# Two attentions on one core: the log-sum rows, spread by VectorE instead of copied by a transfer

## The chip, the cores and the metric

The kernel runs on one core of one Trainium2 chip. The metric is the device time of one execution in microseconds; of several executions the median counts.

## The reference

Two attention layers, A and B, each over its own input x (1 x 2048 x 1024) with its own weights wqkv (1024 x 3072) and wo (1024 x 1024), 32 heads of 32. The results stand side by side in the output.

```python
# A: 8 keys, every second position back          # B: the last 256 positions
off = jnp.arange(8) * 2                          mask = (idx[:, None] - idx[None, :] >= 0) & \
idx = pos[:, None] - off[None, :]                       (idx[:, None] - idx[None, :] < 256)
logits = einsum("bhsd,bhswd->bhsw", q, kg) * scale
attn = softmax(where(mask, logits, -1e9)); o = einsum("bhsw,bhswd->bhsd", attn, vg)
return concatenate([a @ wo_A, b @ wo_B], axis=-1)
```

All is float32. The kernel reaches that precision with matmuls of a shorter format (fp32r) by splitting a number into a high and a low part and adding three products (hi x hi, hi x lo, lo x hi).

## The kernel before, in words

**Units and head groups.** The work is cut into 8 units of 512 positions: four of B ("dense", 256 keys back) and then four of A (its even and odd positions apart, so that its keys are a window of 8 neighbours). Each unit has 8 head groups of 4 heads, 64 head groups in all. The host only lays the arrays out.

**Gemm.** For each unit: q and k of each head group (`qk_items`, matmuls of line 412), the values (`v_items`, line 464) and the output projection (`o_items`, line 510). A weight of 512 KB comes in by a transfer that GpSimd issues (line 137) and is split by VectorE into its two parts (lines 163 and 171) before TensorE reads it.

**Stacked queries and keys.** A finished q or k is evacuated by ScalarE (line 349) and VectorE (line 353) into `nat`, and six transfers issued by SyncE (line 373) place its parts in `qst` and `kst`. There each of the 4 heads has 96 partitions: 32 dimensions times the three pairs of parts, so that one matmul over 96 partitions gives a full-precision score. Two such pairs of tiles alternate between head groups.

**First pass.** Sixteen matmuls a head group (line 681, 4 blocks of 128 queries by 4 heads) give scores with the queries on the partitions. VectorE takes each row's maximum (line 686) and ScalarE the sum of the exponentials (line 691). When all sixteen are done, ScalarE takes the logarithm (line 704), and VectorE makes the negative log-sum and splits it into two parts, `hl` (lines 709 to 712).

**The rows.** The matmul of line 720 turns `hl` round: 32 rows by 128 positions, 16 of high parts and 16 of low parts, row 4j+b (and 16+4j+b) for head j and query block b. VectorE copies them to `rt` (line 724), and a transfer issued by SyncE (line 727) lays them in partitions 96 and 97 of `qst`. `kst` holds ones there, written once at the start (line 285).

**Second pass.** Matmuls over 98 partitions (line 763 in dense units, 566 in the others) give scores with the keys on the partitions, with the log-sum already subtracted by the two extra rows, so that ScalarE's exponential (lines 770 and 573) is the finished softmax. GpSimd or VectorE masks it (lines 749, 752, 583), and the matmuls of lines 810 and 607 multiply by the values. The result is split into `ot` (lines 644 and 648).

**What sets the order.** Nothing is scheduled on the chip. While the program is built, a planner (`Clock`) keeps for each engine the time at which it comes free, books each instruction with a cost written down in the code, and takes from four lists (the rows matmul `aux`, second pass and values `twos`, first pass `ones`, gemm) the item that is ready first, in that order where two are. Each engine then runs its instructions in the order so found, and real semaphores make it wait where the plan was too early. For a transfer the planner books the issue, a move and a tail:

```python
LEAD = dict(sp=1.34, act=0.97, pool=1.43)
MOVE = dict(load=(2.12, 0.14), store=(0.64, 0.4), copy=(1.18, 0.56), rows=(0.37, 0.56), ...
```

A head group's first pass is due when its keys have landed (`done["stack"]`, line 361), its second pass when `h["rows"]` has (line 728). The last step of a q or k gemm waits for an earlier `nat` to be placed, which in turn waits for the second pass of the head group two before, since the stacked tiles are shared. The four PSUM banks of the scores (`rs`) are shared by both passes and the rows.

Of the kernel before, what the change touches and what calls it, by code (L numbers as in the profile page):

```python
# [7 lines left out]
F32 = mybir.dt.float32  # L8
F32R = mybir.dt.float32r
AF = mybir.ActivationFunctionType  # L10
ALU = mybir.AluOpType
# [3 lines left out]
P = 128  # L15
# [6 lines left out]
NRAW, NP, NO, NS = 3, 768, 10, 4  # L22
POOL_BIAS = -99
MASK_BIAS = 0.2
VPARTS = ((0,2),(2,2),(4,2),(6,2))
V_SLOTS = {0: 0, 1: 1, 5: 2, 7: 3}
O_SLOTS = {2: (0, 1), 3: (2, 3), 4: (4, 5), 5: (6, 7)}
V0_SLOTS = {0:0,2:1,4:2,7:3}
NX, NST, NN = 9,1,3
TAIL, XAT = 4, 1  # L30
C1, C3, CG, CV = 0.108, 0.2, 0.231, 0.242
TERMS = ((0, 0), (0, 1), (1, 0))
# [2 lines left out]
class Clock:  # L35
# [4 lines left out]
    SEEN = dict(act=0.15, dve=0.115, pool=0.08)  # L40
    LEAD = dict(sp=1.34, act=0.97, pool=1.43)
    HOLD = dict(sp=0.63, act=0.35, pool=0.6)
    MOVE = dict(load=(2.12, 0.14), store=(0.64, 0.4), copy=(1.18, 0.56), rows=(0.37, 0.56),
                halo_out=(0.4, 0.68), halo_in=(0.55, 0.6), halo_few=(0.28, 0.51))

    def __init__(self):
# [134 lines left out]
def kernel(ctx, tc, xs, wqk, wv, wo, outs, units):  # L181


    nc = tc.nc
    U = len(units)
    ctx.enter_context(tc.manual_schedule())
    const = ctx.enter_context(tc.tile_pool(name="const", bufs=1))
# [6 lines left out]
    small = ctx.enter_context(tc.tile_pool(name="small", bufs=2))  # L194
# [6 lines left out]
    ck = Clock()  # L201
# [28 lines left out]
    for p in plan:  # L230
# [3 lines left out]
        elif p[0] == "v":  # L234
            s0, n = VPARTS[p[2]]
# [25 lines left out]
    def constants():  # L261
        def bands(name, n, keep, fill, *conds):
            m = const.tile([P, n], F32, name=name) if isinstance(name, str) else name
            nc.gpsimd.memset(m, keep)
            for step, base, chan in conds:
                nc.gpsimd.affine_select(m, m, pattern=[[step, n]], compare_op=ALU.is_ge, fill=fill, base=base,
                                        channel_multiplier=chan)
            return m

        ident = cst["ident"] = const.tile([P, P], F32R, name="ident")  # L270
        keep = const.tile([P, P], F32, name="keep_d")
        nc.gpsimd.memset(keep, 0.0)
        nc.gpsimd.affine_select(ident, keep, pattern=[[-1, P]], compare_op=ALU.not_equal, fill=1.0, base=0,
                                channel_multiplier=1)
        cst["mask_d"] = bands("mask_d", 384, 0.0, FAR, (1, -1, -1), (-1, 256, 1))
        cst["mask_w"] = bands("mask_w", 136, 0.0, FAR, (1, -1, -1), (-1, 8, 1))
        cst["keep_f"] = bands("keep_f", P, BIG, 0.0, (-1, -1, 1))
        cst["keep_d"] = bands(keep, P, BIG, 0.0, (1, 0, -1))
        cst["keep_w"] = bands("keep_w", 136, BIG, 0.0, (1, 0, -1), (-1, 7, 1))
        ck.use("pool", 3.0, ck.now)  # L280

        def ones():
            zero = cst["mask_d"][96:98, None, P:2 * P].to_broadcast([2, 24, P])
            for t in kst:
                nc.scalar.activation(t[96:98, :, :].rearrange("p j (a s) -> p (j a) s", s=P), zero, AF.Identity,
                                     bias=1.0, scale=1.0)
                ck.use("act", 2.7, ck.now)

        ck.defer(13.0, ones)
# [39 lines left out]
    def latest(*ts):  # L329
        return None if any(t is None for t in ts) else max(ts)  # L330


    def qk_items(u, s):
# [12 lines left out]
        def evac(t, ps, bank):  # L346
            hl = natp.tile([P, 2, S], F32R, tag="nat", name="nat")
            sc = SCALE if t == 0 else 1.0
            nc.scalar.activation(hl[:, 0, :], ps, AF.Copy, scale=sc)  # L349
            r = ck.use("act", 0.485, ck.now + ck.SEM)  # L350

            def low():
                nc.vector.scalar_tensor_tensor(hl[:, 1, :], ps, sc, hl[:, 0, :].bitcast(F32), op0=ALU.mult,  # L353
                                               op1=ALU.subtract)
                e = ck.use("dve", 0.61, r)
                rg.give(bank, e)

                def stack():
                    e2 = place(1, e)
                    if t == 1:  # L360
                        done["stack"][u, s] = max(e2, h2["hi"])
                    if t == 1 and u + 1 < U and units[u + 1][3]:
                        nc.sync.dma_start(halo[u % 2][s], hl[:, :, 256:].bitcast(F32))
                        e2 = ck.copy("halo_out", e, ck.now)
                    done["nat"][hg, t] = max(e2, h2["hi"])

                later(stack)

            def place(part, e):
                dst, c = (qst[buf], 0) if t == 0 else (kst[buf], 256)  # L370
                for i, a in enumerate((0, 0, 1) if t == 0 else (0, 1, 0)):
                    if a == part:
                        nc.sync.dma_start(dst[i:96:3, :, c:c + S].bitcast(F32), hl[:, a, :].bitcast(F32))
                        e2 = ck.copy("copy", e, ck.now)
                return e2

            def stack_hi():
                if t == 0 and has_halo:
                    read_halo()
                h2["hi"] = place(0, r)  # L380

            def later(f):
                if hg < 2 or hg - 2 in done["second"]:
                    f()
                else:
                    waiting.setdefault(hg - 2, []).append(f)

            h2 = {}
            later(stack_hi)
            ck.defer(r, low)  # L390
# [155 lines left out]
    def window(u, s, h):  # L546
# [12 lines left out]
        def second(ki, hp):  # L559
            kb, q0, n, pack = kbs[ki]  # L560
            if hp == 0:
                h["left", ki] = 4 // pack
            ps, bank = rs.take()
            for i in range(pack):
                j = hp * pack + i
                nc.tensor.matmul(ps[:, i * n:(i + 1) * n], kk[0:98, j, 256 + kb * P:256 + (kb + 1) * P],  # L566
                                 q[0:98, j, q0:q0 + n], start=True, stop=True)
            w = pbuf[:, hp * pack:hp * pack + pack, at[ki]:at[ki] + n]
            if ki == nk - 1 and hp == 4 // pack - 1:
                free_keys(hg)  # L570

            def expo():
                nc.scalar.activation(w, ps[:, :pack * n].rearrange("p (j n) -> p j n", j=pack), AF.Exp)  # L573
                e = ck.use("act", pack * n / 1200 + 0.055, ck.now, pfree[0])
                rs.give(bank, e)

                def masks():
                    if kb < 0:
                        nc.gpsimd.affine_select(w, w, pattern=[[0, pack], [-1, n]], compare_op=ALU.is_ge, fill=0.0,
                                                base=-121, channel_multiplier=1)  # L580
                        r = ck.use("pool", 0.21, e)
                    else:
                        nc.vector.tensor_tensor(w, w, cst["keep_w"][:, None, :n].to_broadcast([P, pack, n]),  # L583
                                                op=ALU.min)
                        r = ck.use("dve", pack * n / 960 + 0.07, e, port=True)
                    h["left", ki] -= 1
                    h["pr", ki] = max(h.get(("pr", ki), 0.0), r)

                ck.defer(e - 0.1, masks)

            return expo
# [25 lines left out]
        def seconds(ki):  # L617
            pack = kbs[ki][3]
            for hp in range(4 // pack):
                two.append(Item(lambda: latest(rs.when(), h["rows"]),  # L620
                                lambda ki=ki, hp=hp: second(ki, hp), pack * C1))

        for ki in range(nk):
# [32 lines left out]
    def attention(u, s):  # L656
# [61 lines left out]
        def rows(hl):  # L718
            ps, bank = rs.take()
            nc.tensor.matmul(ps[0:32, 0:P], hl.rearrange("p a b -> p (a b)"), cst["ident"], start=True, stop=True)  # L720
            rt = small.tile([32, P], F32R, tag="rt", name="rt")

            def copy():
                nc.vector.tensor_copy(rt, ps[0:32, 0:P])
                e = ck.use("dve", 0.2, ck.now)
                rs.give(bank, e)
                nc.sync.dma_start(q[96:98, :, :].bitcast(F32), rt.bitcast(F32))
                h["rows"] = ck.copy("rows", e)

            return copy  # L730

        for b in range(4):
            for j in range(4):
# [21 lines left out]
        def second(ki, hp):  # L755
# [4 lines left out]
                h["left", ki, pr] = 2 // pack  # L760
            ps, bank = rs.take()
            for i, j in enumerate(heads):
                nc.tensor.matmul(ps[:, i * n:(i + 1) * n], kk[0:98, j, 256 + kb * P:256 + (kb + 1) * P],  # L763
                                 q[0:98, j, q0:q0 + n], start=True, stop=True)
            w = pbuf[:, heads[0]:heads[0] + pack, at[ki]:at[ki] + n]
            if ki == nk - 1 and hp == 4 // pack - 1:
                free_keys(hg)
# [20 lines left out]
        def second_ready(ki, hp):  # L788
            pack = kbs[ki][3]
            pr = hp * pack // 2  # L790
            if lot[ki] and ("pv", 0) not in h:
                return None
            return latest(rs.when(), h["rows"])

        def values_ready(ks):
            if ks[-1] == nk - 1 and hg >= NO and ((hg - NO) // NG, NG - 1) not in done["out"]:
# [146 lines left out]
```

## Time and profile before

| What | us |
|---|---|
| median of 3 timed runs | 1946.54 (1946.42 to 1950.07) |
| the profiled execution | 1951.22 |
| its span | 1949.5 |
| TensorE busy | 1904.4 |
| VectorE busy | 1261.6 |
| ScalarE busy | 960.6 |
| GpSimd busy | 375.8 |

The granted TensorE clock was 0.995. The span is what the profiler's records cover; the execution's own time lies 1.7 us above it. Engines: PE is TensorE, PEld its weight loads, DVE VectorE, ACT ScalarE, POOL GpSimd, SP SyncE. A row of the waits names who waited, at which line, for whom, and gives the total, the number of times and the longest. A row of the timeline gives start, duration, engine, line, operation and tiles; the bracket is the idle time ahead of it and what ended it. A row of groups gives the count, then busy time and the mean of one in ns. The records of matmuls that follow each other overlap (a matmul of 512 columns is recorded with 398 ns, while three take 0.74 us), so that an idle time of less than about 0.2 us between two matmuls does not show.

### The profile page before, as it was taken

What the parts mean: (1) busy time and instruction counts of PE and PEld (TensorE: products, weight loads), DVE (VectorE), ACT (ScalarE), POOL (GpSimd) and SP (SyncE); (2) the same over time, 40 slices, a digit from 0 to 9 for tenths busy, and PEclk for the clock granted to TensorE, in tenths of its full rate; (3) what the DMA queues carried; (4) which work ended last, traced back from release to release, by engine and by line L of the source; (5) the groups of instructions that cost most, each with busy time, mean ns of one, the idle gap of its engine ahead of it and who ended that gap; (6) DMA issues with size and microseconds to landing.
All of it is one profiled execution on the core that took longest, in us unless ns stands there. A gap on an engine that the chain in (4) does not pass through costs nothing. (4 is left out here: it accounts for less than half of the span.)

```text
span 1949.5 us, 35937 instructions
## 1 busy us (share of the span) xinstructions
PE 1904.4 (98%) x12608; PEld 1608.6 (83%) x12608; DVE 1261.6 (65%) x3733; ACT 960.6 (49%) x3136; POOL 375.8 (19%) x958
## 2 busy tenths in 40 slices
PE   8999999999999999999999999999999999999999
PEld 6787787788877888778878888888888788888887
DVE  6667566667666676666755667656676566765673
ACT  3555565655565656565655333433444343434441
POOL 1222222323332323232431001000010000000010
PEclk9999999999999999999999999999999999999999
DMA  6456555455545464555454556545564556546451
GB/s 200 131 141 174 134 147 166 136 150 174 144 141 166 133 185 120 144 147 144 134 147 118 173 164 188 157 133 169 148 182 128 169 158 174 167 130 176 138 157 66
DMA packets 136500, 294.90 MB, mean 151 GB/s; under 512 B 14464, under 2 KB 42112, under 8 KB 136320
## 3 DMA queue, kind: packets, MB, share of 16 engines
q1 hardware_dynamic: 85632, 124.82, 26.0%
q0 software_dynamic: 40320, 146.82, 23.2%
q10 hardware_dynamic: 10368, 20.98, 3.0%
q8 instruction: 100, 1.64, 0.4%
q14 instruction: 80, 0.66, 0.1%
HBM read 163.58 MB, written 27.26 MB: 98 GB/s over the span
## 5 line engine op out<-in xcount | busy, mean ns | idle before, releaser
L412 PE MATMUL g<-x,w 128*128 128x512 f32 x3072 | 799.2, 398 | 9.3 <-DVE w L163 9.0
L412 PEld LDWEIGHTS g<-x,w 128*128 128x128 f32 x3072 | 556.9, 189 | 109.3 <-DVE w L163 10.2
L691 ACT ACTIVATE s<-s,nm 128x384 f32<-128x384 f32 (+3 forms) x1024 | 452.2, 442 | 269.1 <-DVE nm L686 261.0
L464 PE MATMUL g<-w,x 128*128 128x256 f32 x3072 | 411.8, 285 | 0.0
L464 PEld LDWEIGHTS g<-w,x 128*128 128x128 f32 x3072 | 392.9, 192 | 2.0 <-issue 0.2
L686 DVE CUSTOM_DVE_ANT_0 s<-s,mask_d 128x384 f32<-128x384 f32 (+2 forms) x512 | 262.4, 555 | 188.5 <-PE s L681 187.7
L510 PE MATMUL g<-ot,w 128*128 128x512 f32 x1416 | 356.7, 396 | 2.7 <-ACT ot L644 2.3
L171 DVE TENSOR_TENSOR w<-raw,w 128x512 fp32r<-128x512 f32 x502 | 328.0, 695 | 8.7
L510 PEld LDWEIGHTS g<-ot,w 128*128 128x128 f32 x1416 | 258.5, 189 | 53.6 <-ACT ot L644 3.3
L749 POOL TENSOR_SCALAR_AFFINE_SELECT pbuf<-pbuf 128x128 f32<-128x128 f32 (+1 forms) x643 | 219.0, 372 | 296.9 <-ACT pbuf L770 295.8
L681 PE MATMUL s<-kst,qst 96*128 96x384 f32 (+3 forms) x1024 | 232.6, 302 | 15.7 <-DMA kst<-nat 9.7
L770 ACT ACTIVATE pbuf<-s 128x384 f32<-128x384 f32 (+2 forms) x480 | 201.9, 503 | 65.8 <-PE s L763 62.6
L681 PEld LDWEIGHTS s<-kst,qst 96*128 96x128 f32 x1024 | 178.4, 190 | 55.6 <-issue 18.2
L686 DVE CUSTOM_DVE_ANT_0 s<-s,mask_w 128x136 f32<-128x136 f32 (+1 forms) x512 | 142.0, 321 | 113.2 <-PE s L681 112.8
L691 ACT ACTIVATION_READ_ACCUMULATOR s<-s,nm 128x1 f32 x1024 | 209.9, 205 | 0.0
L349 ACT ACTIVATE nat<-g 128x512 fp32r<-128x512 f32 x128 | 76.6, 599 | 249.7 <-PE g L412 245.4
L137 POOL DMA_DIRECT2D raw<-wqk x126 | 68.0, 540 | 572.7 <-DVE w L171 218.2
L353 DVE SCALAR_TENSOR_TENSOR nat<-g,nat 128x512 fp32r<-128x512 f32 x128 | 88.3, 690 | 139.1 <-ACT nat L349 136.2
L163 DVE CAST w<-raw 128x1024 fp32r<-128x1024 f32 x251 | 173.1, 690 | 7.3 <-DMA raw<-wqk 7.3
L686 DVE DVE_READ_ACCUMULATOR2_ANT nm<- 128x1 f32 x1024 | 143.7, 140 | 0.0
L763 PEld LDWEIGHTS s<-qst,kst 98*128 98x128 f32 x704 | 109.0, 189 | 40.4 <-ACT s L691 19.6
L583 DVE TENSOR_TENSOR pbuf<-pbuf,keep_w 128x272 f32<-128x272 f32 (+1 forms) x224 | 95.5, 471 | 70.1 <-ACT pbuf L573 69.8
(53 smaller groups left out, 1071.3 us busy)
## 6 DMA issues: line engine op xcount, KB each, us to landing
raw<-wqk POOLq DMA_DIRECT2D x126, 512.0 KB, 3.7
qst<-nat SPq DMA_DIRECT2D x192, 256.0 KB
kst<-nat SPq DMA_DIRECT2D x192, 256.0 KB
raw<-wo POOLq DMA_DIRECT2D x64, 512.0 KB, 3.7
raw<-wv POOLq DMA_DIRECT2D x62, 512.0 KB, 3.7
raw<-xs POOLq DMA_DIRECT2D x28, 512.0 KB, 4.7
outs<-ost ACTq DMA_DIRECT2D x56, 256.0 KB
halo<-nat SPq DMA_DIRECT2D x40, 256.0 KB
```

What stands on the lines that cost most here:

```text
L163: nc.vector.tensor_copy(t[:, 0, :], raw)
L171: nc.vector.tensor_tensor(o, a, b, op=ALU.subtract)
L412: nc.tensor.matmul(h["ps"], h["w"][:, a, k * P:(k + 1) * P], xt[u][k][:, b, :], start=(k == 0 and i == 0), stop=(k == NK - 1 and i == 2))
L464: nc.tensor.matmul(ps, xt[u][k][:, a, p0:p0 + P], h["w"][:, c, k % kw], start=(k == 0 and i == 0 and r == 0), stop=(k == NK - 1 and i == 2 ...
L510: nc.tensor.matmul(h["ps"], w[:, a, c:c + P], ot[u, k][:, b, :], start=(k == 0 and i == 0), stop=(k == NK - 1 and i == 2))
L583: nc.vector.tensor_tensor(w, w, cst["keep_w"][:, None, :n].to_broadcast([P, pack, n]), op=ALU.min)
L681: nc.tensor.matmul(ps[:, :n], q[0:96, j, b * P:(b + 1) * P], kk[0:96, j, c0:c1], start=True, stop=True)
L686: nc.vector.tensor_tensor_reduce(ps[:, :n], ps[:, :n], mask[:, cut:full], scale=-1.0, scalar=BIG, op0=ALU.add, op1=ALU.min, accum_out=nm)
L691: nc.scalar.activation(ps[:, :n], ps[:, :n], AF.Exp, bias=nm, scale=-1.0, accum_out=sm)
L749: nc.gpsimd.affine_select(w, w, pattern=[[0, m], [step, n]], compare_op=ALU.is_ge, fill=0.0, base=base, channel_multiplier=chan)
L763: nc.tensor.matmul(ps[:, i * n:(i + 1) * n], kk[0:98, j, 256 + kb * P:256 + (kb + 1) * P], q[0:98, j, q0:q0 + n], start=True, stop=True)
L770: nc.scalar.activation(w, ps[:, :pack * n].rearrange("p (j n) -> p j n", j=pack), AF.Exp)
```

## The change

VectorE no longer copies the 32 rows, and the transfer is gone. In its place stand four multiplications, one a head, that write 32 rows of `qst` each: all 32 rows of the matmul's result, repeated over the 4 query blocks, times a small table `pick` that is 1 where a row belongs to the head and the block and 0 elsewhere. `kst` holds ones in 32 partitions instead of 2, and the second pass runs over all 128 partitions. The second pass of a head is due in the plan when that head's multiplication is done, instead of when all rows have landed. `ROWS_LATE`, added to that time, is 0. `KEYS_LATE` adds 1.2 us to the time at which the planner takes the keys to have landed. As the planner's times change, so does the order of the instructions on every engine.

```diff
+ROWS_LATE, KEYS_LATE = 0, 1.2
...
+        pick = cst["pick"] = const.tile([32, 16], F32, name="pick")
+        nc.gpsimd.memset(pick, 0.0)
+        for row in (0, 16):
+            nc.gpsimd.affine_select(pick, pick, pattern=[[-1, 16]], compare_op=ALU.not_equal, fill=1.0, base=-row,
+                                    channel_multiplier=1)
...
-            zero = cst["mask_d"][96:98, None, P:2 * P].to_broadcast([2, 24, P])
+            zero = cst["mask_d"][96:P, None, P:2 * P].to_broadcast([32, 24, P])
             for t in kst:
-                nc.scalar.activation(t[96:98, :, :].rearrange("p j (a s) -> p (j a) s", s=P), zero, AF.Identity,
+                nc.scalar.activation(t[96:P, :, :].rearrange("p j (a s) -> p (j a) s", s=P), zero, AF.Identity,
...
-                        done["stack"][u, s] = max(e2, h2["hi"])
+                        done["stack"][u, s] = max(e2, h2["hi"]) + KEYS_LATE
...
-                nc.tensor.matmul(ps[:, i * n:(i + 1) * n], kk[0:98, j, 256 + kb * P:256 + (kb + 1) * P],
-                                 q[0:98, j, q0:q0 + n], start=True, stop=True)
+                nc.tensor.matmul(ps[:, i * n:(i + 1) * n], kk[:, j, 256 + kb * P:256 + (kb + 1) * P],
+                                 q[:, j, q0:q0 + n], start=True, stop=True)
...
-                two.append(Item(lambda: latest(rs.when(), h["rows"]),
+                two.append(Item(lambda hp=hp: latest(rs.when(), h["rows"] and h["rows"][hp * pack + pack - 1]),
...
-            rt = small.tile([32, P], F32R, tag="rt", name="rt")
-
-            def copy():
-                nc.vector.tensor_copy(rt, ps[0:32, 0:P])
-                e = ck.use("dve", 0.2, ck.now)
+            def spread():
+                h["rows"] = []
+                for j in range(4):
+                    nc.vector.tensor_tensor(q[96:P, j, :].rearrange("p (b s) -> p b s", s=P),
+                                            ps[0:32, None, 0:P].to_broadcast([32, 4, P]),
+                                            cst["pick"][0:32, 4 * j:4 * j + 4, None].to_broadcast([32, 4, P]), op=ALU.mult)
+                    e = ck.use("dve", 0.61, ck.now)
+                    h["rows"].append(e + ROWS_LATE)
                 rs.give(bank, e)
-                nc.sync.dma_start(q[96:98, :, :].bitcast(F32), rt.bitcast(F32))
-                h["rows"] = ck.copy("rows", e)
```

The dense second pass is changed in the same two places.

More of the change, by code (lines that the diff above doesn't have):

```diff
@@ L28 @@
 V0_SLOTS = {0:0,2:1,4:2,7:3}
-NX, NST, NN = 9,1,3
+NX, NST, NN = 9, 1, 3
 TAIL, XAT = 4, 1
@@ L42 @@
     HOLD = dict(sp=0.63, act=0.35, pool=0.6)
-    MOVE = dict(load=(2.12, 0.14), store=(0.64, 0.4), copy=(1.18, 0.56), rows=(0.37, 0.56),
+    MOVE = dict(load=(2.12, 0.14), store=(0.64, 0.4), copy=(1.18, 0.56),
                 halo_out=(0.4, 0.68), halo_in=(0.55, 0.6), halo_few=(0.28, 0.51))
@@ L720, in rows @@
             nc.tensor.matmul(ps[0:32, 0:P], hl.rearrange("p a b -> p (a b)"), cst["ident"], start=True, stop=True)
-            rt = small.tile([32, P], F32R, tag="rt", name="rt")
-            def copy():
-                nc.vector.tensor_copy(rt, ps[0:32, 0:P])
-                e = ck.use("dve", 0.2, ck.now)
+            def spread():
[6 more added lines that the diff above has]
+                    h["rows"].append(e + ROWS_LATE)
                 rs.give(bank, e)
-                nc.sync.dma_start(q[96:98, :, :].bitcast(F32), rt.bitcast(F32))
-                h["rows"] = ck.copy("rows", e)
-            return copy
+            return spread
         for b in range(4):
@@ L762, in second @@
             for i, j in enumerate(heads):
-                nc.tensor.matmul(ps[:, i * n:(i + 1) * n], kk[0:98, j, 256 + kb * P:256 + (kb + 1) * P],
-                                 q[0:98, j, q0:q0 + n], start=True, stop=True)
+                nc.tensor.matmul(ps[:, i * n:(i + 1) * n], kk[:, j, 256 + kb * P:256 + (kb + 1) * P],
+                                 q[:, j, q0:q0 + n], start=True, stop=True)
             w = pbuf[:, heads[0]:heads[0] + pack, at[ki]:at[ki] + n]
@@ L792, in second_ready @@
                 return None
-            return latest(rs.when(), h["rows"])
+            return latest(rs.when(), h["rows"] and h["rows"][hp * pack + pack - 1])
         def values_ready(ks):
```

## The prediction

> **What bounds the kernel now.** I read the page's first two parts, then the waits of TensorE alone, then the timeline around the longest of them.
>
> ```profile
> span 1949.5 us, 35937 instructions
> PE 1904.4 (98%) x12608; PEld 1608.6 (83%) x12608; DVE 1261.6 (65%) x3733; ACT 960.6 (49%) x3136; POOL 375.8 (19%) x958
> ```
>
> TensorE is busy for 1904.4 of 1949.5 us; no other engine is near its span. The change takes no matmul away, so it can only act on the 45.1 us in which TensorE is idle. The first matmul and the last row of the trace bound the two ends:
>
> ```profile
> 8.06 7.18 PE L412 MATMUL g<-x,w 128*128 128x512 f32 x19 [8.06 <-DVE w L163]
> ...
> 1945.97 0.58 ACT L428 COPY pbuf<-g 128x512 f32<-128x512 f32 x1 [4.85 <-PE g L510]
> ```
>
> 8.1 us pass before the first matmul, and about 3.5 us (1949.5 - 1946.0) after the last one. Neither end is touched. Some 33 us of idle time remain in the middle, and the waits of TensorE name them (total us, times, longest):
>
> ```profile
> PE s L681 <- DMA kst<-nat: 9.7, 6, 2.5
> PE g L412 <- DVE w L163: 9.0, 3, 8.1
> PE s L763 <- DMA qst<-rt: 5.3, 4, 1.8
> PE s L681 <- ACT s L691: 5.2, 5, 1.6
> PE s L566 <- DMA qst<-rt: 3.0, 3, 1.7
> PE g L510 <- ACT ot L644: 2.3, 3, 0.8
> PE s L720 <- DVE hl L712: 1.9, 3, 0.6
> ```
>
> The two rows with qst<-rt are the transfer that the change removes: 5.3 + 3.0 = 8.3 us in 7 of 64 head groups. The first row is the keys, which the change's second constant concerns: 9.7 us, 6 times. Together they are 18.0 us, 0.9% of the span. That is the most that the change can give by what it says.
>
> **The removed transfer.** One of the seven stalls in full:
>
> ```profile
> 80.91 0.22 PE L720 MATMUL s<-ident,hl 128*32 128x128 f32 x1
> 82.09 0.27 DVE L724 CAST rt<-s 32x128 fp32r<-32x128 f32 x1
> 82.39 0.68 SPq L727 DMA_DIRECT2D qst<-rt  x1
> 86.75 0.42 PE L763 MATMUL s<-qst,kst 98*128 98x384 f32 x1 [1.80 <-DMA qst<-rt]
> ```
>
> From the issue to the matmul that reads the rows it is 4.36 us. The planner books 1.34 + 0.37 + 0.56 = 2.27 us for it, some 2.1 us too few. In most groups gemm work stands in between and hides the error; in seven it doesn't. With the transfer gone this error is gone: -8.3 us. On SyncE's own queue the transfer also stood ahead of others while it waited for the cast:
>
> ```profile
> SPq L727 <- DVE rt L724: 198.3, 42, 22.7
> ```
>
> What stands behind it are the copies of queries and keys for the next head group but one, and the halo reads; these wait for the second pass of this one, which comes later still. So the freed queue gives 0. VectorE's cast also gives up its time:
>
> ```profile
> L724 DVE CAST rt<-s x64: 269/279/279, 53.2 to 1902.4; 32x128 fp32r<-32x128 f32 x64
> L648 DVE TENSOR_TENSOR ot<-o,ot 128x512 fp32r<-128x512 f32 x64 | 44.0, 687 | 28.7 <-ACT ot L644 28.7
> 985.73 0.69 DVE L353 SCALAR_TENSOR_TENSOR nat<-g,nat 128x512 fp32r<-128x512 f32 x1
> 986.33 0.56 DVE L686 CUSTOM_DVE_ANT_0 s<-s,mask_d 128x384 f32<-128x384 f32 x1
> ...
> 986.81 0.69 DVE L648 TENSOR_TENSOR ot<-o,ot 128x512 fp32r<-128x512 f32 x1
> 987.41 0.56 DVE L686 CUSTOM_DVE_ANT_0 s<-s,mask_d 128x384 f32<-128x384 f32 x1
> ```
>
> **The added work.** Four multiplications of 32 x 512 stand for one cast. No row has that shape; the nearest is L648, which also reads PSUM and one SBUF tile and writes 512 elements of fp32r a partition: 687 ns, with the next instruction starting 0.60 us after it, as behind L353. So four take 4 x 0.60 = 2.4 us of the queue (bounds: 2.4, and 4 x 0.69 = 2.76 if they don't overlap). The planner books 4 x 0.61 = 2.44, which is right for the lower bound. Over 64 groups VectorE gains 64 x 4 x 0.687 = 176 us of busy time and loses 64 x 0.28 = 18. In the changed order 30 more masks stand on VectorE and 30 fewer on GpSimd, at 0.294 us each (row below) about 9 us more. That makes some 1429 us, 73% of the span: still no bound.
>
> ```profile
> L752 DVE TENSOR_TENSOR pbuf<-pbuf,keep_d 128x128 f32<-128x128 f32 x33 | 9.7, 294 | 8.7 <-ACT pbuf L770 8.6
> ```
>
> Does it reach TensorE later than the transfer did? In the stall above the cast started at 82.09. In its place the first multiplication would end at 82.8 and the last at 82.09 + 3 x 0.60 + 0.69 = 84.6, against 86.75. Even the last head's rows come 2 us sooner, and TensorE waits for them head by head. The planner knows this, and it puts less gemm in between. A row of the chain of waits gives the price of gemm:
>
> ```profile
> 1539.56 2.12 PE g L510 x9
> ```
>
> At 0.23 us for 512 columns and half of it for 256, the changed order has some 2 us of gemm between the L720 matmul and the first second-pass matmul in many groups (14 of 64 under 2.2 us, 37 under 3, the least 1.4; in the order before the median was 5.2). So the cover is thinner, and lateness of VectorE shows at once.
>
> How late may VectorE be? An undisturbed hand-over from L720 to VectorE:
>
> ```profile
> 503.90 0.22 PE L720 MATMUL s<-ident,hl 128*32 128x128 f32 x1
> 504.16 0.28 DVE L724 CAST rt<-s 32x128 fp32r<-32x128 f32 x1 [0.77 <-PE s L720]
> ```
>
> 0.26 us, then 0.69: the first rows are there 1.0 us after the matmul starts. With a weight split ahead, as at 80.91, it is 1.18 + 0.69 = 1.9 us, just inside the usual cover. Chains that stay on the chip are planned well now: L720 waited for VectorE's hl 3 times in 64 groups, 1.9 us. For four such hand-overs a group I take +3 us. The bounds are 0 and 64 x 4 x (0.69 - 0.60) = 23 us, if nothing overlaps and every delay reaches TensorE. The value is near the lower end, because the row of the same kind is.
>
> The block is also the only work of VectorE that writes from partition 96 on; all other outputs start at 0. The trace of before has no such step, so whether the overlap of 0.69 - 0.60 = 0.09 us holds across its two edges is open: nothing, or 64 x 2 x 0.09 = 12 us of VectorE's time, half of it ahead of the first rows. The nearest rows (L353 and L648 above) overlap, so the sum takes nothing, and the other end is a rival. [...]
>
> **Second-pass matmuls over 128 rows instead of 98.**
>
> ```profile
> L681 PE MATMUL s<-kst,qst 96*128 96x384 f32 x448 | 126.8, 351 | 3.5 <-ACT s L691 3.3
> L763 PE MATMUL s<-qst,kst 98*128 98x384 f32 x256 | 68.1, 350 | 4.1 <-DMA qst<-rt 4.1
> L464 PE MATMUL g<-w,x 128*128 128x256 f32 x3072 | 411.8, 285 | 0.0
> L763 PE MATMUL s<-qst,kst 98*128 98x256 f32 x224 | 41.2, 288 | 0.0
> ```
>
> 351 at 96 rows, 350 at 98; 285 at 128 rows, 288 at 98. Rows cost nothing: 0. The ones written to 32 partitions and the small table on GpSimd belong to the first microseconds, long before the first L763: 0.
>
> **Keys 1.2 us later in the plan.** The six stalls:
>
> ```profile
> 184.88 0.63 PE L681 MATMUL s<-kst,qst 96*128 96x128 f32 x4 [2.53 <-DMA kst<-nat]
> 220.01 0.63 PE L681 MATMUL s<-kst,qst 96*128 96x128 f32 x4 [1.92 <-DMA kst<-nat]
> 1024.80 0.63 PE L681 MATMUL s<-kst,qst 96*128 96x128 f32 x4 [1.04 <-DMA kst<-nat]
> 1043.68 0.52 PE L681 MATMUL s<-kst,qst 96*128 96x128 f32 x3 [2.04 <-DMA kst<-nat]
> 1464.06 0.63 PE L681 MATMUL s<-kst,qst 96*128 96x128 f32 x4 [0.46 <-DMA kst<-nat]
> 1536.39 0.63 PE L681 MATMUL s<-kst,qst 96*128 96x128 f32 x4 [1.70 <-DMA kst<-nat]
> ```
>
> The transfers themselves don't get faster; gemm work comes ahead of the matmul instead. If they land as they do now, each stall shrinks by up to 1.2: 1.20 + 1.20 + 1.04 + 1.20 + 0.46 + 1.20 = 6.3 us, and 3.4 stay. The bounds are 0 and 9.7.
>
> The price is attention that starts later. In the changed order of the first unit there are two long stretches without gemm instead of one (values, eight second-pass and four first-pass matmuls, values), and behind one of them three more first-pass matmuls that need banks still held by ScalarE. Those are three times some 0.7 us (L686's 0.56 + 0.14), partly under the values: +2 us, between 0 and 4.
>
> What stays: TensorE's wait around 980 us, where a weight came late to VectorE:
>
> ```profile
> 983.32 0.69 DVE L163 CAST w<-raw 128x1024 fp32r<-128x1024 f32 x1 [7.30 <-DMA raw<-wqk]
> ```
>
> **The sum.** -8.3 - 6.3 + 2 + 3 = -9.6 us. The profiled execution took 1951.22 us, 1.7 more than its span, so it would take 1941.6. The median of the three timed runs is 1946.54, 4.7 lower; I take the same difference from it: **1937 us**.
>
> **The rivals.**
> First, VectorE becomes late. Each group's 2.4 us block holds up the maxima (L686) behind it and with them the four banks of the first pass, and the thin cover lets lateness through. With the non-overlapping price of 23 us in place of 3, the sum is -8.3 - 6.3 + 2 + 23 = +10.4: 1957. It decides the sign from 12.6/64 = 0.20 us of lateness a group. For it: 73% busy, in bursts, and 37 groups with under 3 us of cover. Against it: the 0.60 spacing is what the planner books.
> Second, the stalls move on. The row stalls go, but the reordered plan meets other late transfers (keys, weights) as often, as the one before did in 6 + 1 places: 0 to -3 us, 1945.
> Third, the block loses the overlap at its edges. The first rows come 0.09 us later in each group, 6 us if all of it reached TensorE; I count half, since gemm in blocks of three (0.7 us) lies ahead of the waiting matmul: 1940. The edge behind the block meets maxima that have 27% of idle time to catch up in.
> Fourth, it doesn't do what it says: TensorE waits for all four multiplications. Then three more, 1.8 us, come off a gain of some 2 to 4 us a group, the cover of 2 us is too thin in many groups, and some 6 us of the 9.6 are lost: 1943. The order shows the waits on VectorE head by head, so it is unlikely.
>
> **How the numbers follow.** The forecast has 0.50, lost edges 0.06, VectorE late 0.22, stalls that move 0.18, all four awaited 0.04. 0.2% is 3.9 us, about what a measurement of this kernel tells from no change: faster means below 1942.6, slower above 1950.4. So faster 0.50 + 0.06 = 0.56, same 0.18 + 0.04 = 0.22, slower 0.22. The range starts where all 18.0 us go and nothing comes (1928.5) and ends just short of the late VectorE's full price, at 1955. The forecast's own range is 1929 to 1942.
>
> **What would show it.** In the waits of TensorE no row names qst<-rt; the kst<-nat row is near 3 us; rows from VectorE's new line are together under 5 us. The new instruction is near 690 ns and spaced 0.60 in its group; if it is 0.69 or more apart, the first rival is at work, and waits for L686, for ScalarE's banks or for the new line have grown past 15 us. The forecast is wrong if TensorE's busy time differs from 1904 by more than 4 us, or if weights (L163, L171) become a releaser of gemm in the middle of the run.

## The result, and the profile after

Median of 4 executions before: 1947.35 us (1946.42 to 1950.07); of 4 after: 1929.66 us (1929.00 to 1931.76). The ratio is 0.9909, with a 95% interval of 0.9892 to 0.9926: 17.7 us less, where 9.6 were forecast (the time itself lies 7 us below the forecast 1937, in the range and 1.2 us above its lower end). Two executions of the experiments, one at about a quarter of the usual speed and one 6% longer at a granted clock of 0.848, are in none of the figures.

The first two parts of the page after:

```profile
span 1928.3 us, 36059 instructions
PE 1899.9 (99%) x12608; PEld 1609.0 (83%) x12608; DVE 1412.6 (73%) x3956; ACT 962.3 (50%) x3135; POOL 378.3 (20%) x931
```

TensorE still bounds the kernel, with as many matmuls as before. VectorE went from 1261.6 to 1412.6 us, and no wait of TensorE names its new line. The waits of TensorE after, all but four rows of together 1.3 us (total us, times, longest):

```profile
PE g L418 <- DVE w L164: 8.2, 1, 8.2
PE s L726 <- DVE hl L718: 4.5, 4, 3.5
PE s L687 <- ACT s L697: 3.9, 4, 1.6
PE s L726 <- ACT s L697: 2.3, 3, 1.0
PE s L772 <- ACT s L697: 1.8, 3, 0.6
PE g L516 <- ACT ot L650: 1.6, 2, 0.8
```

The numbers of the lines have moved: 418 was 412, 687 was 681, 697 was 691, 726 was 720, 772 was 763, and 732 is the new one. The two rows with qst<-rt are gone, and so is the row with kst<-nat; none names L732, the multiplications. From before to after: rows' transfer -8.3, keys -9.7, the weight L164 -0.8, the log-sum `hl` +2.6, all waits for ScalarE's line 697 (691 before) together +0.2 (7.8 to 8.0), the rest about -1.

Three numbers of each profiled execution give the whole. The span is the idle time of TensorE (span less busy time), plus the time lost to a lowered clock ((1 - clock) x span; the clock has three digits, so this is known to 1 us, and a lowered clock during a wait counts too), plus the rest, which is the work at full clock.

| | span | idle | lost to the clock | rest |
|---|---|---|---|---|
| before | 1949.5 | 45.1 | 9.7 | 1894.7 |
| after | 1928.3 | 28.4 | 7.7 | 1892.2 |
| difference | -21.2 | -16.7 | -2.0 | -2.5 |

So the idle time carries it. (The profiled execution of before lies 3.9 us above its median, that of after 0.3; hence -21.2 here and -17.7 between the medians.)

### The profile page after: what moved, and what is told of

It reads as the page before. It is cut to its first block, busy times and chain, and to the rows that moved or that the text cites. A ratio compares the mean times of both kernels' runs of the same rounds, so it can differ in the third digit from the quotient of the medians.

```text
span 1928.3 us, 36059 instructions
## 1 busy us (share of the span) xinstructions
PE 1899.9 (99%) x12608; PEld 1609.0 (83%) x12608; DVE 1412.6 (73%) x3956; ACT 962.3 (50%) x3135; POOL 378.3 (20%) x931
## 4 chain that ended last, share of the span: by engine, by line
PE 96%; DVE 2%; ACT 1%; DMA 1%; issue 0%; ACTq 0%; DVEq 0%
PE g L418 37%; PE g L470 19%; PE g L516 18%; PE s L687 7%; PE s L772 5%; PE o L819 4%; PE s L572 3%; PE o L613 2%; ACT s L697 1%; DMA raw<-xs 0%; PE s L516 0%; DMA qst<-nat 0%; DVE w L172 0%; DVE s L692 0%; PE s L726 0%
## 5 line engine op out<-in xcount | busy, mean ns | idle before, releaser
L687 PE MATMUL s<-kst,qst 96*128 96x384 f32 (+3 forms) x1024 | 238.6, 302 | 4.9 <-ACT s L697 3.9
L732 DVE TENSOR_TENSOR qst<-s,pick 32x512 fp32r<-32x512 f32 x256 | 158.4, 675 | 39.3 <-PE s L726 38.4
L164 DVE CAST w<-raw 128x1024 fp32r<-128x1024 f32 x251 | 174.2, 694 | 0.4
L772 PEld LDWEIGHTS s<-qst,kst 128*128 128x128 f32 x704 | 111.2, 189 | 35.9 <-ACT s L697 11.9
```

Source lines behind the costliest of these rows:

```text
L164: nc.vector.tensor_copy(t[:, 0, :], raw)
L687: nc.tensor.matmul(ps[:, :n], q[0:96, j, b * P:(b + 1) * P], kk[0:96, j, c0:c1], start=True, stop=True)
L732: nc.vector.tensor_tensor(q[96:P, j, :].rearrange("p (b s) -> p b s", s=P), ps[0:32, None, 0:P].to_broadcast([32, 4, P]), cst["pick"][0:32 ...
L772: nc.tensor.matmul(ps[:, i * n:(i + 1) * n], kk[:, j, 256 + kb * P:256 + (kb + 1) * P], q[:, j, q0:q0 + n], start=True, stop=True)
```

## The experiments

**The theories.** The *stall theory* is that of the prediction: waits for the rows and for the keys are gone, each worth its length, and nothing of like size came. Its rival is the *order theory*: any change of the planner's times gives another order on every engine, another order has other waits, and the gain lies in the order that this change happened to get, not in the rows or the keys.

Each ratio below is to executions of before that were taken with the run (their medians were 1950.6 to 1952.1 us). The change itself was measured only against the four of the section above (1947.35), so its ratio can be set beside the others to some 0.2% only.

### Each half alone

The spread alone (the change with the first edit, measured twice) and the later keys alone (before with the second):

```diff
-ROWS_LATE, KEYS_LATE = 0, 1.2
+ROWS_LATE, KEYS_LATE = 0, 0.0
```

```diff
-                        done["stack"][u, s] = max(e2, h2["hi"])
+                        done["stack"][u, s] = max(e2, h2["hi"]) + 1.2
```

> The spread by VectorE with KEYS_LATE at 0. Theory of stalls (the gain is the two kinds of stall, rows 8.3 us and keys 9.7 us): no wait on the rows, a wait on kst<-nat of 5 to 10 us, time 1936 to 1940 where the whole change gave 1929.7. Theory of scatter (every new order of the instructions moves the time by some 10 us whatever is changed): the waits do not add up to the difference, and the time may lie anywhere from 1925 to 1950.

> The spread without the keys' 1.2 us once more, for a profile. Theory of stalls: a wait on kst<-nat of 5 to 10 us and nothing on the rows. Theory of feedback (a later first pass or second pass holds up the placing of nat, on which the last step of a q or k gemm waits, so that TensorE has no gemm left to fill with at the turn of a unit): kst<-nat small too, since the keys' wait of before belonged to its order, and the difference to the changed kernel stands in waits on hl and ScalarE near the turns at about 460, 720 and 980 us.

> The kernel before with 1.2 us added to the keys' time, transfer kept. Theory of stalls: kst<-nat falls from 9.7 to under 4 us, qst<-rt stays at 6 to 10 us, time 1937 to 1942. Theory of scatter: qst<-rt and other waits move by as much as the keys' wait falls, 1940 to 1955.

Measured: the spread alone 0.9935 [0.9918, 0.9952] and 0.9943 [0.9924, 0.9963], the keys alone 0.9938 [0.9922, 0.9955]. Each half is worth some 0.6%, 12 us; both together 0.9%, not 1.2%. The waits of TensorE with the keys alone:

```profile
PE s L763 <- DMA qst<-rt: 3.5, 4, 1.9
...
PE s L566 <- DMA qst<-rt: 2.8, 6, 0.7
...
PE s L681 <- DMA kst<-nat: 1.0, 1, 1.0
```

The keys' wait falls from 9.7 to 1.0, as the stall theory wants. The rows' transfer is still waited for, 10 times and 6.3 us, and VectorE's copy of the rows (line 724) once, 2.7 us. With the spread alone:

```profile
PE s L687 <- DMA kst<-nat: 4.7, 2, 2.9
PE s L772 <- DVE qst L732: 4.7, 1, 4.7
PE s L572 <- DVE qst L732: 4.7, 3, 1.6
```

No transfer of rows is left to wait for, but VectorE's multiplications are: 9.4 us in four places, more than the 8.3 that the transfer had cost. At the turns of the units TensorE waits as long as in the change (1.03 us each against 0.93), although the feedback theory, in the expectation of the second run, wanted the difference there. One of the four waits for the multiplications:

```profile
218.34 0.66 PE L772 MATMUL s<-qst,kst 128*128 128x384 f32 x1 [4.67 <-DVE qst L732]
```

With the keys booked 1.2 us later, all four are gone. The two constants of the change are not two separate gains: each sets the order in which the other's waits fall.

### The transfer kept, and booked as it is

If the gain is the planner's error on the transfer, then it is enough to book the transfer at the 4.36 us that the trace shows, and to leave it where it is:

```diff
-    MOVE = dict(load=(2.12, 0.14), store=(0.64, 0.4), copy=(1.18, 0.56), rows=(0.37, 0.56),
+    MOVE = dict(load=(2.12, 0.14), store=(0.64, 0.4), copy=(1.18, 0.56), rows=(0.37, 2.65),
```

> The kernel before with the rows' transfer kept and booked at 4.36 us after its issue instead of 2.27, as the trace shows it. Theory of stalls: the gemm is there to fill the time, so the wait on the rows goes and the time is 1937 to 1941, as good as the spread without the keys. Theory of earliness (the second pass has to come early, because what follows it, key copies and values, is late next): the wait on the rows goes, but others grow, 1943 to 1955.

Measured 1.0027 [1.0014, 1.0040], 1956.9 us: slower than before, and a little over what the theory of earliness allowed. The waits of TensorE:

```profile
PE s L720 <- DVE hl L712: 8.3, 4, 2.3
PE s L681 <- DMA kst<-nat: 8.3, 7, 2.6
...
PE s L681 <- DMA kst<-halo: 3.5, 1, 3.5
```

No row names qst<-rt. The wait that was aimed at is gone altogether, 8.3 us of it, and the kernel is about 5 us slower: `hl` went from 1.9 to 8.3, halo transfers came in with 5.4 (3.5 and, in another row, 1.9). Here the stall theory, "gone and nothing came", fails. A wait that the plan foresees is no delay taken away: nothing in this edit makes the rows land sooner, and what comes behind them in the plan is put later. Three of the four `hl` waits stand at the turns of the dense units, at 477, 742 and 1000 us (1.25 us of waiting for ScalarE ahead of two of them):

```profile
986.69 0.45 PE L681 MATMUL s<-kst,qst 96*128 96x384 f32 x1 [1.25 <-ACT s L691]
999.70 0.22 PE L720 MATMUL s<-ident,hl 128*32 128x128 f32 x1 [2.30 <-DVE hl L712]
```

### Rows booked later, with the spread in place

This led to a third theory, the *feedback*: the last step of a k gemm waits for an earlier `nat` to be placed, that placing waits for the second pass of an earlier head group, and the second pass waits for the rows. Rows that are due later hold up the gemm at the turn of a unit, until TensorE has none left and waits for `hl` in the open. By it, a later `ROWS_LATE` alone must bring those waits back and cost more the later it is:

```diff
-ROWS_LATE, KEYS_LATE = 0, 1.2
+ROWS_LATE, KEYS_LATE = 2.0, 1.2
```

and the same with 1.0 and with 0.3.

> The changed kernel with ROWS_LATE at 2.0: the rows are as early as in it, but the plan places the second pass 2 us later, about where it stood with the transfer. Theory of stalls: 1928 to 1932, as the changed kernel. Theory of earliness: 1934 or more, with waits on ScalarE's banks, values or keys grown.

> ROWS_LATE at 1.0, between the changed kernel (0) and 2.0 (ratio 0.9943). Theory of feedback: the wait on hl at the three turns of a unit lies between 0.3 us and 1.7 us each, and the ratio to before between 0.991 and 0.9945. Theory of scatter: no such order; either may lie outside by more than 0.3%.

> The changed kernel with ROWS_LATE at 0.3, which covers the lost overlap at the edges of VectorE's block (2 x 0.09 us) and little more. Theory of stalls: no wait on the rows was left, so the plan has nothing to gain and the ratio is 0.989 to 0.993. Theory of scatter: a new order, anywhere from 0.988 to 1.003.

| `ROWS_LATE` | ratio, interval | idle | lost to the clock | waits for `hl` |
|---|---|---|---|---|
| 0 (the change) | 0.9909 [0.9892, 0.9926] | 28.4 | 7.7 | 4.5 |
| 0.3 | 0.9898 [0.9882, 0.9914] | 33.8 | 7.7 | 8.4 |
| 1.0 | 1.0026 [1.0016, 1.0037] | 38.8 | 15.6 | 10.8 |
| 2.0 | 0.9943 [0.9925, 0.9960] | 36.4 | 9.7 | 7.4 |

The waits at the turn come back in all three, but not in proportion: 1.0 is worse than 2.0, and 0.3, which has at each turn the 1.25 and 2.30 us that the kernel with the booked transfer has at two, is as fast as the change. 2.0 came out as the theory of earliness in its expectation wanted (1940 us), 0.3 as that of stalls did; 1.0 lies outside what the feedback theory allowed, in its waits and in its ratio. As a law of dose, the feedback theory fails. At 1.0, the gain of the change is lost entirely, by one constant and with the same instructions (some two dozen of them moved to GpSimd, by the planner's choice). The turn there:

```profile
980.62 1.01 PE L687 MATMUL s<-kst,qst 96*128 96x384 f32 x2 [1.25 <-ACT s L697]
994.58 0.22 PE L726 MATMUL s<-ident,hl 128*32 128x128 f32 x1 [2.86 <-DVE hl L718]
```

and the same place in the change:

```profile
974.44 0.82 PE L772 MATMUL s<-qst,kst 128*128 128x128 f32 x4 [0.60 <-ACT s L697]
...
983.02 0.22 PE L726 MATMUL s<-ident,hl 128*32 128x128 f32 x1 [0.32 <-DVE hl L718]
```

In the change SyncE issues the transfers of the queries 7.7 us ahead of the rows matmul (975.32), with 1.0 only 6.2 us ahead of it (988.33), and the idle time of the turn is 0.92 against 4.11 us. There are three such turns: 9.6 of the 10.4 us of idle time by which the two differ.

### One gemm step moved at the turn

If the turn's wait comes from the last step of the eighth k gemm, then it goes when that step is moved four items back, into the values' gemm behind it, so that other gemm work stands ahead of it:

```diff
+            if V_SLOTS.get(NG - 1) == p[2]:
+                new[4:4] = [gemm.pop()]
```

This was put into the kernel with `ROWS_LATE` 1.0, and into the change.

> ROWS_LATE at 1.0 (ratio 1.0026) with one edit: at the turn of a unit the last step of the eighth k gemm, which waits for nat, stands four steps (24 matmuls, some 2.9 us) into the value gemm that follows, so that TensorE has gemm while it waits. Theory of feedback (the gemm runs out because its last step waits for the placing of nat, and that for the second pass): the waits at 450 to 480, 720 to 740 and 980 to 1000 us (1.25 + 2.86 each) fall under 1.5 us a turn, ratio 0.993 to 0.998. Theory of scatter: the waits fall elsewhere and the ratio stays within 0.2% of 1.0026 or moves either way.

> The changed kernel (ratio 0.9909) with the same edit. Theory of feedback: it has only 0.9 us of wait left at each of three turns, so at most 3 us are to be had: ratio 0.989 to 0.992. Theory of scatter: anywhere from 0.987 to 1.0.

With 1.0: 0.9975 [0.9963, 0.9986] in place of 1.0026. The long waits are gone at the first two turns (one of 0.60 us is left), and stand as they were at the third:

```profile
954.06 0.86 PE L418 MATMUL g<-x,w 128*128 128x512 f32 x3
...
987.30 0.22 PE L726 MATMUL s<-ident,hl 128*32 128x128 f32 x1 [2.86 <-DVE hl L718]
987.36 1.34 PE L418 MATMUL g<-x,w 128*128 128x512 f32 x3
```

The first row is the moved step: it stands behind 18 matmuls of the values, as at the first turn (440.68), so the edit acts at the third turn too, and the wait does not go. Nor is the moved step the one at the wait. In the kernel with 1.0 that was not edited, 48 matmuls of 512 columns, the q and k gemm of one head group, lie between the end of the values (972.99) and the end of the step right behind the waiting rows matmul (994.63). The step at the wait, here at 987.36, is therefore the last of the next unit's first k gemm, 33 us behind the moved one. What the edit shows is that the waits of two turns went when the order ahead of them became another; that the moved step was their cause is not shown, and the step at the wait itself was moved in no run. In the change itself the same edit loses the gain: 0.9989 [0.9978, 1.0000], where the feedback theory wanted 0.989 to 0.992. Two long waits appeared at other places:

```profile
180.51 1.49 PE L819 MATMUL o<-pbuf,vbuf 128*32 128x256 f32 x12 [4.02 <-DVE pbuf L761]
...
1894.14 0.69 PE L687 MATMUL s<-kst,qst 96*128 96x136 f32 x2 [3.09 <-ACT s L697]
```

and the clock lost 17.5 us instead of 7.7. One step moved at each turn, no instruction added, and the time rises by 0.8%, though no wait for L732 came back. That is what the order theory says of this kernel.

### Is it the order alone?

Then spread and transfer should do equally well once the order is varied. The keys were booked at 2.4 us in both, in the change by the first edit and in before by the second:

```diff
-ROWS_LATE, KEYS_LATE = 0, 1.2
+ROWS_LATE, KEYS_LATE = 0, 2.4
```

```diff
-                        done["stack"][u, s] = max(e2, h2["hi"])
+                        done["stack"][u, s] = max(e2, h2["hi"]) + 2.4
```

> KEYS_LATE at 2.4 instead of 1.2. Theory of stalls: nothing is left to take away (the wait on kst<-nat was gone at 1.2), so 1928 to 1933. Theory of feedback: the later first pass delays all that follows, 1934 to 1942, with waits at the turns of the units grown.

> The kernel before, transfer kept, keys booked 2.4 us later: the third pair (transfer against spread) beside 0 us (1.0 against 0.9935 and 0.9943) and 1.2 us (0.9938 against 0.9909); the spread has 0.9912 here. If the spread itself gives something at every booking of the keys: 0.994 to 1.0. If order alone decides: as likely below 0.9912 as above.

| keys booked later by | with the transfer | with the spread |
|---|---|---|
| 0 | 1 (before) | 0.9935 [0.9918, 0.9952], 0.9943 [0.9924, 0.9963] |
| 1.2 | 0.9938 [0.9922, 0.9955] | 0.9909 [0.9892, 0.9926] |
| 2.4 | 1.0005 [0.9996, 1.0015] | 0.9912 [0.9894, 0.9931] |

At each of the three the spread is the faster, by 0.6, 0.3 and 0.9%. With the transfer and 2.4 the waits for the rows rise:

```profile
PE s L566 <- DMA qst<-rt: 8.8, 11, 2.0
...
PE s L763 <- DMA qst<-rt: 1.8, 3, 0.8
```

10.6 us at 14 places, against 0.7 us for L732 with the spread and the same 2.4. With a transfer that is booked too short, every order so far left 6 to 11 us of waiting for the rows; with the spread booked as it runs, four of the five orders with `ROWS_LATE` 0 or 0.3 left under 1 us, and one 9.4. So there is more to it than the order, it seems, but these pairs don't show it: if the order alone decided, one of the two would be ahead in all three pairs one time in four, and at 1.2 the two intervals touch. The two expectations weren't met to the letter either: with the spread the time is 1934.4 us, between the two theories, and the waits for `hl` have not grown (3.5 us), and the transfer's 1.0005 lies just above the range that was given for a spread that helps at every booking.

### The multiplications made twice

This tests how much lateness of VectorE the plan can hide, which the prediction's first rival needs. Each multiplication is issued twice, and the planner books it once, so that the order stays:

```diff
-                    nc.vector.tensor_tensor(q[96:P, j, :].rearrange("p (b s) -> p b s", s=P),
+                    for _ in range(2):
+                        nc.vector.tensor_tensor(q[96:P, j, :].rearrange("p (b s) -> p b s", s=P),
```

> The changed kernel with each of the four multiplications made twice (the same values written again), the plan unchanged: VectorE 2.4 us late in each head group. Theory that cover is thin (first rival of the prediction): TensorE waits for the new line in most groups, 1 to 2 us each, 1990 to 2050. Theory that VectorE has room (27% idle) and gemm hides it: under 20 us longer, 1932 to 1950.

Measured 1.0772 [1.0746, 1.0798], 150 us over before and more than even the theory of a thin cover expected (1990 to 2050 us). The waits of TensorE (the multiplications are at line 733 here):

```profile
PE s L773 <- DVE qst L733: 47.0, 63, 2.3
PE s L572 <- DVE qst L733: 44.9, 53, 2.2
```

What VectorE was made late by is 64 x 4 x 0.60 = 154 us; the span grew by 166 over the change's. Of that 92 are these 116 waits, 43 more were lost to the clock, which fell to 0.976, and some 28 stand in the rest, where the trace doesn't place them. Little is hidden: 60 of the 64 head groups wait, 1.5 us in the mean of the 2.4 by which they are late. That there is no L732 among the waits of the change is hardly because the plan has slack; four multiplications take about what is booked (2.48 us against 2.44).

## Why the prediction was right, and where its sizes were off

**The forecast as a whole.** The kind was right: the two kinds of stall that were aimed at went, and nothing of their size came. The size was not: -17.7 us for -9.6. That the time fell in the range at all has luck in it. Other bookings of the same kernel gave 1932 to 1957 us, and the sum has no term that tells one order from another.

**The bound.** Right: TensorE, with only its idle time to win. Its busy time is 4.1 us below the 1904 that the prediction named, with the same 12608 matmuls, and 4 was the limit beyond which it called itself wrong. That sign was set too narrowly: a matmul at half clock counts as busy (after, 2.00 us of the 2 between 218 and 220 at a clock of 0.50), about 2 us of it are the clock (9.7 to 7.7), and over the experiments that add no work the busy time lies between 1898.1 and 1913.4 us.

**The removed transfer, -8.3.** Both rows are gone, as they must be without the transfer. But the step "with the transfer gone this error is gone" held for the time only in the order that came with it. Booking the transfer as it runs removes the same wait and costs 5 us, and the spread without the later keys lost 9.4 us to waits of its own.

**The added work.** The groups and the block's spacing:

```profile
L732 DVE TENSOR_TENSOR qst<-s,pick 32x512 fp32r<-32x512 f32 x256 | 158.4, 675 | 39.3 <-PE s L726 38.4
L772 PE MATMUL s<-qst,kst 128*128 128x384 f32 x256 | 67.8, 350 | 0.0
```

675 ns for one, 687 forecast; four take 2.48 us, so they start (2.48 - 0.675)/3 = 0.60 us apart, as taken from L648. VectorE is 73% busy, as worked out, though 16 us less than the 1429: the prediction counted four full records of 0.687 us a group, and as they overlap the 64 blocks take 158.4 us, not 176. The term for late hand-overs was +3 and measured 0 in the change. It depends on the order: 0 with 0.3 us, 0.7 with the keys at 2.4, 9.4 with the keys at 0, all inside the bounds of 0 to 23. The doubled multiplications bear out the first rival's price, about a microsecond for each that VectorE is late (166 for 154); its trigger, a spacing of 0.69, was absent.

**The edges of the block.** The third rival's mechanism is there. Two places of VectorE's timeline, an SBUF output behind the block, and a PSUM output behind another one:

```profile
302.85 2.48 DVE L732 TENSOR_TENSOR qst<-s,pick 32x512 fp32r<-32x512 f32 x4 [1.16 <-PE s L726]
305.36 0.69 DVE L164 CAST w<-raw 128x1024 fp32r<-128x1024 f32 x1
```

```profile
137.69 2.47 DVE L732 TENSOR_TENSOR qst<-s,pick 32x512 fp32r<-32x512 f32 x4
140.09 0.41 DVE L692 CUSTOM_DVE_ANT_0 s<-s,mask_d 128x256 f32<-128x256 f32 x1
```

The cast starts at 305.36, 0.03 after the block's end at 305.33: no overlap. The maximum starts at 140.09, 0.07 before the block's end at 140.16: overlap kept. So it is in all 31 places where an SBUF output follows a block without idle time (0.02 to 0.04 us after its end) and in all 19 where a PSUM output does (0.06 to 0.08 before it). The cast of line 164 behind line 359, both from partition 0, starts 0.08 us before the end (at 56.04, the end at 56.12). Ahead of a block it is the same: behind an SBUF output from partition 0 that ended at 190.14 the block starts at 190.17. What decides whether the overlap is lost or kept no run tested. The lost overlap cost TensorE nothing in the change's order: no wait for L732 came of it.

**128 rows instead of 98.** Right: 350 ns at 384 columns as before.

**The keys, -6.3.** The mis-sized term: -9.7 measured. It was worked out as if each stall shrank by the 1.2 us of the booking and 3.4 us stayed. The likely reason, not followed stall by stall: the booking doesn't push a matmul back by 1.2 us, but makes the planner put whole pieces of gemm ahead of it (three matmuls of 512 columns are 0.7 us), and the order of all that follows is another. With the keys alone 1.0 stays, with both 0.

**The price of later attention, +2.** About right in kind and too large. The two stretches without gemm cost 1.0 us in all:

```profile
172.44 0.44 PE L772 MATMUL s<-qst,kst 128*128 128x128 f32 x2 [0.33 <-ACT pbuf L779]
...
176.57 0.44 PE L687 MATMUL s<-kst,qst 96*128 96x384 f32 x1 [0.69 <-ACT s L697]
```

**What was said to stay.** TensorE's wait around 980 us did not: 1.08 + 1.57 + 0.65 = 3.3 us between 979 and 987 before, 0.60 + 0.32 = 0.92 after, and VectorE's wait for the weight (7.3 us at L163) is 0.4 at L164. A transfer's arrival was taken as fixed while the plan around it moved.

**What was not in the sum.** One new wait, 3.50 us for `hl` at 215.52, and the clock. The total: idle -16.7 in place of -9.6, the clock -2.0 and the rest -2.5 in place of 0.

**What stays open.** How much of the 0.9% belongs to the spread and how much to the order it happened to get is open. The three pairs say 0.3 to 0.9% for the spread; single moves of the order are worth up to 1.2% (from 0.9909 to 1.0026). Why `ROWS_LATE` 1.0 is worse than 2.0 was followed only to the turns of the units, and what sets the waits there is open: the feedback theory failed as a law of dose, and the step that was moved is not the one at the wait. A fourth `nat` buffer, which by that theory would cut the feedback at its root, wasn't tried. The rest, the work at full clock, isn't constant either: leaving out the doubled multiplications, it lies between 1890 and some 1900 us with the same matmuls, and nothing here says why.

## What to carry to other kernels

In a kernel whose order is planned ahead, a stall that is removed is worth its length only if the new order has no other in its place: read the waits of the whole run after the change, not only the row that was aimed at, and compare the two designs at several bookings before a gain under 1% is put down to the design. Booking a step as it runs is not enough by itself: the transfer, booked at its 4.36 us, was waited for no longer, and the kernel was slower. And where an engine's work is planned to the tenth, there is little slack behind it: of 154 us by which VectorE was made late 92 stood open as waits, and with the lowered clock and the rest the run grew by 166.

## What the runs showed of the hardware

**A wait, and half clock behind it.** Stretches of before, behind the wait of 2.04 us that ended at 1043.68 (window, its length, TensorE's busy time with its instructions, granted clock, DMA share, GB/s):

```profile
1042.00:1044.00 2.00, 0.32 (x3) 1.00 0.32 108
1044.00:1046.00 2.00, 2.00 (x12) 0.57 0.83 260
1046.00:1048.00 2.00, 2.00 (x13) 0.58 0.02 6
```

and of after, behind the wait of 3.50 us:

```profile
215.52 0.29 PE L726 MATMUL s<-ident,hl 128*32 128x128 f32 x1 [3.50 <-DVE hl L718]
```

```profile
214.00:216.00 2.00, 0.48 (x3) 0.60 1.07 299
216.00:218.00 2.00, 2.00 (x11) 0.50 0.33 83
218.00:220.00 2.00, 2.00 (x12) 0.50 0.54 176
220.00:222.00 2.00, 2.00 (x13) 0.70 0.22 86
```

In the first, 2 x (0.43 + 0.42) = 1.7 us were lost, some 3.4 us at half clock; in the second the clock was at half for 2 x 2 x (0.40 + 0.50 + 0.50 + 0.30) = 6.8 us, twice as long, of which about 1.1 us fell into the wait itself and 5.7 cost 2.8 us of work. All such stretches ahead of the last matmul have one of these two lengths: in before three of 3.4 us (between 220 and 226, 1044 and 1048, 1220 and 1226) and one of 6.8 (1896 to 1906), in after two of 6.8 (214 to 222, 1876 to 1884). A wait of 0.97 us (before, at 1219.59) was followed by half clock too, one of 2.53 us (before, at 184.88) by none:

```profile
184.00:186.00 2.00, 1.12 (x10) 1.00 1.07 417
...
1222.00:1224.00 2.00, 2.00 (x7) 0.50 0.12 49
```

So the length of the wait alone doesn't decide whether the clock falls, and no run here shows what does. With the doubled multiplications the lowered clock cost 43 us more than in the change (0.976 of a span of 2094.6 us, against 0.996 of 1928.3), and the 116 waits that came in were none of them over 2.3 us.
